# The second attention read in float32, one head per 32 columns of TensorE

## The chip, the cores and the metric

The kernel runs on one core of a Trainium2 chip. The time is device time in microseconds (us) of one execution. A core has TensorE (PE in the profile; its weight loads are PEld), VectorE (DVE), ScalarE (ACT), GpSimd (POOL) and SyncE (SP), whose queue issues the DMAs. Each engine has its own list of instructions and runs it in order; semaphores hold an instruction until what it needs is done.

## The reference

An attention between a sequence x and a small state, in both directions, and then a feed-forward layer:

```python
B, H, S, Ns, D = 8, 8, 512, 32, 64
a = softmax(scale * x @ state.T)          # over the 32 state rows
xread = a @ state
a2 = softmax(scale * state @ x.T)         # over the 512 positions
sread = a2 @ x                            # the second read: 32 x 64 per head
attn = concatenate([xread, sread], axis=2)
h = relu(attn_as_rows @ w_in)             # 512 -> 2048
out = (h * h) @ w_out                     # 2048 -> 512
```

attn_as_rows has 8 x 544 = 4352 rows of 8 heads x 64 = 512. All is float32 outside; w_in and w_out come as float64 and are decoded on the chip.

## The kernel before

**Blocks.** There are nine blocks of rows: block b from 0 to 7 holds the 512 x-read rows of batch b, block 8 the 256 state-read rows of all batches. For a block, hidden (16 steps) makes 128 of the 2048 hidden features each, and accumulate (16 steps) multiplies them by w_out into four accumulators in PSUM, one per 128 rows (tag acc, four buffers; two for block 8, from another pool). The state is multiplied into w_in beforehand, so hidden takes the softmax itself (k) as its moving operand.

**Split operands.** Most matmuls take operands in the type float32r as a high part (a cast on ACT) and a low part (a subtraction on DVE or POOL, as the table SECOND says); mm3 then adds three products, high by high, high by low and low by high. Blocks 0 and 1 (b < NX = 2) do parts of the attention in plain float32 instead.

**The second read.** A batch has two groups g of four heads, with 4 x 32 = 128 state rows on the partitions. For a group:

- scores: the scores in PSUM, with the four heads' states as a block-diagonal stationary operand; exp_s: e2, the exponentials (128 x 512), with the row sums, and r2, the reciprocals of the sums.
- load_n: loads x of the four heads with positions on the partitions (xn, tag xp, two buffers) and, for b >= 2, splits it into xn_hi and xn_lo (tags x_hi and x_lo, one buffer each, which prep uses too). There the buffer of xn is free when the split is done.
- transposes: four PE transposes of e2 into PSUM (pt, pool ps_b with two buffers), then to SBUF: a float32 copy eT for b < 2, a split into eT_hi and eT_lo for the others.
- sread: four position slices k. The stationary operand is the slice of eT (128 positions x 128 rows, four heads side by side), the moving one all four heads of xn (256 columns). The result pr is 128 x 256, of which only the four diagonal blocks (head by the same head) are used. For b < 2 these are four float32 matmuls, for the others mm3 with twelve. Four scalings by r2 on ACT pick the diagonal blocks into srd, and a DVE transpose writes them to srall, the input of block 8.

**The order.** The text PLAN lists the steps; a step's instructions are issued in that order, and the framework's scheduler (`TileContext(nc, schedule_with_timeline_sim=True)`) then writes each engine's list by estimates of durations, so that an engine's list may depart from the plan. A tile with a tag waits for one of that tag's buffers. The tag xp has two buffers, shared by x for prep (load), by xn (load_n), by the partial sums of blocks 0 and 1 (load_part, one tile for accumulators 0 and 1, one for 2 and 3), and at the end by half of the weights of block 8 (load_wi). These DMAs are issued from SP's queue. For block 1 the plan has load_n.2.0, load_n.2.1, sread.2.0, load_part.1, sread.2.1 and then the last two accumulates of block 1, whose sums are added to the parts in store (L812).

Of the kernel before, what the change touches and what calls it, by code (L numbers as in the profile page):

```python
# [10 lines left out]
F32 = mybir.dt.float32  # L11
F32R = mybir.dt.float32r
# [206 lines left out]
def tile_attn_moe(  # L219
# [31 lines left out]
    nc = tc.nc  # L251

    w_in_w, w_out_w = w_in.bitcast(U32), w_out.bitcast(U32)
    B, H, S, D = x.shape
# [3 lines left out]
    P = 128  # L258
# [7 lines left out]
    NX = 2  # L266
    LAG = 2
    second = set()
    for line in SECOND.replace("\n        ", " ").split("\n"):
        kind, _, keys = line.strip().partition(": ")  # L270
# [4 lines left out]
    KC = S // P  # L275

    cp = ctx.enter_context(tc.tile_pool(name="cp", bufs=1))
    p2 = ctx.enter_context(tc.tile_pool(name="p2", bufs=2))
    ps_acc = ctx.enter_context(tc.tile_pool(name="ps_acc", bufs=4, space=bass.MemoryType.PSUM))
    ps_h = ctx.enter_context(tc.tile_pool(name="ps_h", bufs=2, space=bass.MemoryType.PSUM))  # L280
    ps_b = ctx.enter_context(tc.tile_pool(name="ps_b", bufs=2, space=bass.MemoryType.PSUM))
# [17 lines left out]
    def pick(key, *engs):  # L299

        return engs[key in second]

    def split(hi, lo, src, key):

        nc.scalar.copy(hi, src)  # L305
        pick(key, nc.gpsimd, nc.vector).tensor_sub(lo, src, hi.bitcast(F32))  # L306

    def split_v(hi, lo, src):
        nc.scalar.copy(hi, src)
        nc.vector.tensor_sub(lo, src, hi.bitcast(F32))  # L310

    def evac(key, out, src):
        if key in second:
            nc.vector.tensor_copy(out, src)
        else:
            nc.scalar.copy(out, src)
# [5 lines left out]
    def mm3(ps, pairs, first=True, last=True, pin=False, skip=False):  # L322

        seq = []
        for (lh, ll), (rh, rl) in pairs:
            seq += [(lh, rh), (lh, rl), (ll, rh)]
        for i, (l, r) in enumerate(seq):
            m = nc.tensor.matmul(  # L328
                ps, l, r, start=first and i == 0, stop=last and i == len(seq) - 1, skip_group_check=skip
            )  # L330
            if pin:
                tc.keep_in_program_order(m)
# [29 lines left out]
    class Attention:  # L362
# [113 lines left out]
        def load_n(self, g):  # L476
            b = self.b
            x_v = x[b, 4 * g : 4 * g + 4].rearrange("h (p k) d -> p h (k d)", k=KC)
            if b < NX:
                xn = p2.tile([P, KC, 4, D], F32, tag="xp", name=f"xn{b}_{g}")  # L480
                for k in range(KC):
                    nc.sync.dma_start(xn[:, k], x_v[..., D * k : D * k + D])
                self.xn[g] = xn
                return
            xn = p2.tile([P, 4, KC, D], F32, tag="xp", name=f"xn{b}_{g}")
            nc.sync.dma_start(xn.rearrange("p h k d -> p h (k d)"), x_v)
            xnhi = p2.tile([P, 4, KC, D], F32R, tag="x_hi", name=f"xn_hi{b}_{g}", bufs=1)
            xnlo = p2.tile([P, 4, KC, D], F32R, tag="x_lo", name=f"xn_lo{b}_{g}", bufs=1)
            split(xnhi, xnlo, xn, f"xn_lo.{b}.{g}")
            self.xn[g] = (xnhi, xnlo)  # L490

        def transposes(self, g):
            b, e2 = self.b, self.e2.pop(g)
            pt = ps_b.tile([P, KC, P], F32, tag="psb", name=f"pt{b}_{g}")
            for k in range(KC):
                nc.tensor.transpose(pt[:, k], e2[:, k], ident)  # L496
            if b < NX:
                eT = p2.tile([P, KC, P], F32, tag="eT_hi", name=f"eTf{b}_{g}", bufs=1)
                evac(f"eT.{b}.{g}", eT, pt)
                self.eT[g] = eT  # L500
                return
            eThi = p2.tile([P, KC, P], F32R, tag="eT_hi", name=f"eT_hi{b}_{g}", bufs=1)
            eTlo = p2.tile([P, KC, P], F32R, tag="eT_lo", name=f"eT_lo{b}_{g}", bufs=1)
            split_v(eThi, eTlo, pt)
            self.eT[g] = (eThi, eTlo)

        def sread(self, g):

            b = self.b
            eT, xn, r2 = self.eT.pop(g), self.xn.pop(g), self.r2.pop(g)  # L510
            pr = ps_b.tile([P, 4, D], F32, tag="psb", name=f"pr{b}_{g}")
            prf = pr.rearrange("p h d -> p (h d)")
            if b < NX:
                for k in range(KC):
                    nc.tensor.matmul(prf, eT[:, k], xn[:, k].rearrange("p h d -> p (h d)"), start=k == 0, stop=k == KC - 1)
            else:
                mm3(
                    pr,
                    [((eT[0][:, k], eT[1][:, k]), (xn[0][:, :, k], xn[1][:, :, k])) for k in range(KC)],
                )  # L520
            srd = p2.tile([P, 2, 32], F32, tag="srd", name=f"srd{b}_{g}")
            for h in range(4):
                q = slice(32 * h, 32 * h + 32)
                nc.scalar.mul(srd[q].rearrange("p e d -> p (e d)"), pr[q, h], r2[q])  # L524
            nc.vector.transpose(srall[:, 2 * g : 2 * g + 2, b * Ns : b * Ns + Ns], srd)


# [465 lines left out]
    for k in PLAN.split():  # L993
        f, args, after = steps[k]
# [34 lines left out]
```

## Time and profile before

| | us |
|---|---|
| runs of the kernel (3) | 718.09, 719.53, 720.15; median 719.53 |
| the profiled execution | 718.72 |
| its span (first to last instruction) | 716.9 |
| granted clock of TensorE, mean share of full | 0.993 |

The profile is of one execution. A group of instructions is named by line, engine, operation and out<-in, with buffer numbers left out. Matmuls are pipelined and their ends are modelled: the starts say more than the durations. L328 is the matmul in mm3 and stands for many uses, so the tile's name tells them apart; pr is the second read's result.

| second read, before | instructions | first to last start, us |
|---|---|---|
| matmuls, blocks 0 and 1 (L515) | 32, 128x256 | 23.3 to 138.7 |
| matmuls, blocks 2 to 7 (L328, three products) | 3 x 48, 128x256 | 197.8 to 584.9 |
| scalings on ACT (L524) | 64, 32x64 | 26.7 to 586.1 |

### The profile page before, as it was taken

How to read it: one execution, taken by the hardware profiler on the slowest of the kernel's cores; microseconds unless marked ns; L12 is line 12 of the kernel's file. 1: busy time of each engine (PE TensorE's matmuls, PEld its weight loads, DVE VectorE, ACT ScalarE, POOL GpSimd, SP SyncE). 2: the span in 40 equal slices, each digit the busy share in tenths (PEclk: the TensorE clock that was granted, in tenths of full speed). 3: DMA queues.
4: the chain of work that ended last, by engine and by line, in shares of the span. 5: the costliest groups of instructions: out<-in, count | busy, mean ns of one | idle time of the engine just before them, and what ended most of it. 6: DMA issues, size and time to landing. Idle time of an engine off the chain costs nothing.

```text
span 716.9 us, 9806 instructions
## 1 busy us (share of the span) xinstructions
PE 688.5 (96%) x3281; PEld 571.7 (80%) x3281; DVE 422.0 (59%) x745; ACT 407.7 (57%) x798; POOL 145.0 (20%) x132
## 2 busy tenths in 40 slices
PE   5789699999999999999999999999999999999997
PEld 4567488878788888878888888888888888888886
DVE  4899989699665666766635574467348332322232
ACT  4586855777675656547645565557456553334323
POOL 1221601334202324423320230114003010000000
PEclk9999899999999999999999999999999999999999
DMA  9836477655765443565516354554355234434402
GB/s 274 218 105 222 154 250 240 214 181 160 256 193 182 164 161 104 189 203 170 166 49 203 103 164 156 195 176 162 89 176 160 75 102 141 141 113 115 126 0 89
DMA packets 94866, 113.64 MB, mean 159 GB/s; under 512 B 25952, under 2 KB 64864, under 8 KB 94816
## 3 DMA queue, kind: packets, MB, share of 16 engines
q1 hardware_dynamic: 94816, 113.02, 50.2%
q8 instruction: 26, 0.43, 0.3%
q14 instruction: 24, 0.20, 0.1%
HBM read 70.52 MB, written 42.47 MB: 158 GB/s over the span
## 4 chain that ended last, share of the span: by engine, by line
PE 79%; DVE 7%; DMA 6%; ACT 3%; issue 2%; SPq 2%; POOL 1%; DVEq 0%; ACTq 0%; POOLq 0%
PE acc L328 45%; PE ph L328 24%; PE pr L328 2%; PE st L328 2%; DMA wo_raw<-in_moe_w_out_dram 2%; PE w2ps L328 2%; DMA out_dram<-o 1%; PE qps L728 1%; PE qps L729 1%; DMA w_f<-w2p_d 1%; DMA xp<-in_x_dram 1%; SPq L685 1%; DVE dec L344 1%; DMA wi_raw<-in_moe_w_in_dram 1%; PE pt L496 1%
## 5 line engine op out<-in xcount | busy, mean ns | idle before, releaser
L328 PE MATMUL acc<-wo,g_hi 128*128 128x512 f32 x1088 | 315.9, 392 | 0.7 <-ACT g_hi L786 0.5
L328 PEld LDWEIGHTS acc<-wo,g_hi 128*128 128x128 f32 x1088 | 201.9, 188 | 42.3 <-ACT g_hi L786 0.9
L328 PE MATMUL acc<-wo,g_lo 128*128 128x512 f32 x544 | 187.9, 391 | 0.0
L328 PE MATMUL ph<-k_hi,w 128*128 128x512 f32 x512 | 181.6, 395 | 5.7 <-DVE g_lo L791 5.6
L791 DVE TENSOR_TENSOR g_lo<-ph,g_hi 128x512 fp32r<-128x512 f32 (+1 forms) x140 | 91.6, 655 | 102.7 <-ACT g_hi L786 101.4
L328 PEld LDWEIGHTS ph<-k_hi,w 128*128 128x128 f32 x512 | 96.5, 189 | 27.6 <-DVE g_lo L791 7.4
L328 PEld LDWEIGHTS acc<-wo,g_lo 128*128 128x128 f32 x544 | 101.0, 188 | 19.8
L786 ACT CAST g_hi<-ph 128x512 fp32r<-128x512 f32 (+1 forms) x144 | 81.1, 564 | 42.8 <-DVE ph L785 32.3
L328 PE MATMUL ph<-k_lo,w 128*128 128x512 f32 x256 | 100.5, 393 | 0.0
L785 DVE SCALAR_TENSOR_TENSOR ph<-ph,r 128x512 f32<-128x512 f32 (+1 forms) x76 | 49.9, 656 | 70.2 <-ACT r L784 70.2
L784 ACT ACTIVATE r<-ph 128x512 f32<-128x512 f32 (+1 forms) x76 | 43.1, 567 | 74.7 <-PE ph L328 74.3
L780 ACT ACTIVATE ph<-ph 128x512 f32<-128x512 f32 (+1 forms) x68 | 38.5, 568 | 53.2 <-PE ph L328 52.6
L328 PEld LDWEIGHTS ph<-k_lo,w 128*128 128x128 f32 x256 | 48.6, 190 | 9.2
L306 POOL TENSOR_TENSOR w<-w_f,w 128x512 fp32r<-128x512 f32 x23 | 30.1, 1309 | 93.0 <-ACT w L305 89.8
L781 ACT ACTIVATE ph<-ph 128x512 f32<-128x512 f32 (+1 forms) x68 | 38.6, 569 | 1.2
L306 POOL TENSOR_TENSOR x_lo<-xT,x_hi 128x512 fp32r<-128x512 f32 x11 | 14.3, 1303 | 111.1 <-ACT x_hi L305 99.0
L305 ACT CAST w<-w_f 128x512 fp32r<-128x512 f32 x40 | 24.6, 616 | 10.5 <-DMA w_f<-w2p_d 6.0
L622 PE MATMUL w2ps<-dec,bd 128*128 128x256 f32 x64 | 17.2, 419 | 11.6 <-DVE dec L344 8.6
L524 ACT ACTIVATE srd<-pr,r 32x64 f32<-32x64 f32 x64 | 19.6, 306 | 12.3 <-PE pr L328 9.5
L328 PE MATMUL ph<-sr_hi,s 128*128 128x256 f32 x128 | 25.5, 282 | 0.0
L622 PEld LDWEIGHTS w2ps<-dec,bd 128*128 128x128 f32 x64 | 12.9, 209 | 15.0 <-ACT bd L552 8.3
L306 POOL TENSOR_TENSOR xn_lo<-xn,xn_hi 128x1024 fp32r<-128x1024 f32 x7 | 16.8, 2400 | 36.1 <-ACT xn_hi L305 32.2
(134 smaller groups left out, 919.4 us busy)
## 6 DMA issues: line engine op xcount, KB each, us to landing
wi_raw<-in_moe_w_in_dram SPq DMA_DIRECT2D x16, 512.0 KB, 4.6
wo_raw<-in_moe_w_out_dram SPq DMA_DIRECT2D x16, 512.0 KB, 5.2
w_d<-qo SPq DMA_DIRECT2D x64, 128.0 KB, 2.1
out_dram<-o SPq DMA_DIRECT2D x32, 256.0 KB, 3.3
w_f<-w_d SPq DMA_DIRECT2D x32, 256.0 KB, 3.2
win_d<-wi SPq DMA_DIRECT2D x16, 512.0 KB, 3.3
w<-w2a_d SPq DMA_DIRECT2D x32, 256.0 KB, 3.9
s<-win_d SPq DMA_DIRECT2D x128, 64.0 KB, 2.0
```

What stands on the lines that cost most here:

```text
L305: nc.scalar.copy(hi, src)
L306: pick(key, nc.gpsimd, nc.vector).tensor_sub(lo, src, hi.bitcast(F32))
L328: m = nc.tensor.matmul(ps, l, r, start=first and i == 0, stop=last and i == len(seq) - 1, skip_group_check=skip)
L344: nc.vector.scalar_tensor_tensor(v, low, 29, v, ALU.logical_shift_right, ALU.bitwise_or)
L524: nc.scalar.mul(srd[q].rearrange("p e d -> p (e d)"), pr[q, h], r2[q])
L622: nc.tensor.matmul(ps[:, b], bd_f[b][:, 2 * g + c], w[:, c], start=first_c, stop=c == 1, skip_group_check=True)
L780: nc.scalar.activation(ph, ph, AF.Relu)
L781: nc.scalar.activation(ph, ph, AF.Square)
L784: nc.scalar.activation(r, ph, AF.Relu)
L785: nc.vector.scalar_tensor_tensor(ph, ph, 0.0, r, ALU.max, ALU.mult)
L786: nc.scalar.copy(ghi, ph)
L791: nc.vector.tensor_sub(glo, ph, ghi.bitcast(F32))
```

## The change

Three parts, for all blocks alike:

- load_n no longer splits xn: the float32 tile itself is kept for the read.
- transposes ends with one float32 copy eT (on ACT, or on DVE where SECOND lists it: 0.1 and 1.0 alone) for all blocks.
- sread makes, for each slice k and each head h, one float32 matmul: 32 columns of eT stationary, the 64 columns of that head moving, into the 32 partitions of pr that belong to the head. tile_position=(0, 32 * h) puts each into its own 32 columns of the array. pr is now 128 x 64, and one scaling by r2 takes the place of four.

```diff
-            xnhi = p2.tile([P, 4, KC, D], F32R, tag="x_hi", name=f"xn_hi{b}_{g}", bufs=1)
-            xnlo = p2.tile([P, 4, KC, D], F32R, tag="x_lo", name=f"xn_lo{b}_{g}", bufs=1)
-            split(xnhi, xnlo, xn, f"xn_lo.{b}.{g}")
-            self.xn[g] = (xnhi, xnlo)
+            self.xn[g] = xn
...
-            if b < NX:
-                eT = p2.tile([P, KC, P], F32, tag="eT_hi", name=f"eTf{b}_{g}", bufs=1)
-                evac(f"eT.{b}.{g}", eT, pt)
-                self.eT[g] = eT
-                return
-            eThi = p2.tile([P, KC, P], F32R, tag="eT_hi", name=f"eT_hi{b}_{g}", bufs=1)
-            eTlo = p2.tile([P, KC, P], F32R, tag="eT_lo", name=f"eT_lo{b}_{g}", bufs=1)
-            split_v(eThi, eTlo, pt)
-            self.eT[g] = (eThi, eTlo)
+            eT = p2.tile([P, KC, P], F32, tag="eT_hi", name=f"eT{b}_{g}", bufs=1)
+            evac(f"eT.{b}.{g}", eT, pt)
+            self.eT[g] = eT
...
-            pr = ps_b.tile([P, 4, D], F32, tag="psb", name=f"pr{b}_{g}")
-            prf = pr.rearrange("p h d -> p (h d)")
-            if b < NX:
-                for k in range(KC):
-                    nc.tensor.matmul(prf, eT[:, k], xn[:, k].rearrange("p h d -> p (h d)"), start=k == 0, stop=k == KC - 1)
-            else:
-                mm3(
-                    pr,
-                    [((eT[0][:, k], eT[1][:, k]), (xn[0][:, :, k], xn[1][:, :, k])) for k in range(KC)],
-                )
+            pr = ps_b.tile([P, D], F32, tag="psb", name=f"pr{b}_{g}")
+
+            for k in range(KC):
+                for h in range(4):
+                    q = slice(32 * h, 32 * h + 32)
+                    xh = xn[:, k, h] if b < NX else xn[:, h, k]
+                    nc.tensor.matmul(pr[q], eT[:, k, q], xh, start=k == 0, stop=k == KC - 1, tile_position=(0, 32 * h))
             srd = p2.tile([P, 2, 32], F32, tag="srd", name=f"srd{b}_{g}")
-            for h in range(4):
-                q = slice(32 * h, 32 * h + 32)
-                nc.scalar.mul(srd[q].rearrange("p e d -> p (e d)"), pr[q, h], r2[q])
+            nc.scalar.mul(srd.rearrange("p e d -> p (e d)"), pr, r2)
             nc.vector.transpose(srall[:, 2 * g : 2 * g + 2, b * Ns : b * Ns + Ns], srd)
```

## The prediction

> **What bounds the kernel now.** I read the page's busy shares first, then the table by stretches, then the waits.
>
> ```profile
> span 716.9 us, 9806 instructions
> PE 688.5 (96%) x3281; PEld 571.7 (80%) x3281; DVE 422.0 (59%) x745; ACT 407.7 (57%) x798; POOL 145.0 (20%) x132
> PE 79%; DVE 7%; DMA 6%; ACT 3%; issue 2%; SPq 2%; POOL 1%; DVEq 0%; ACTq 0%; POOLq 0%
> ```
>
> The first line is the span, the second busy time by engine, the third the chain that ended last by engine. TensorE (PE) is busy 96% of the span and is 79% of the chain. A share is an average over stages, so the table by stretches comes next: length, then busy time and instructions of PE, its weight loads (PEld), DVE, ACT and POOL, then granted clock and DMA.
>
> ```profile
> 0.00:60.00 60.00, 44.69 (x180) 32.73 (x181) 46.39 (x101) 37.36 (x84) 12.90 (x18) 0.97 0.72 208
> 60.00:185.00 125.00, 117.35 (x527) 95.35 (x526) 109.63 (x196) 88.90 (x173) 38.47 (x36) 0.97 0.60 198
> 185.00:590.00 405.00, 403.26 (x1947) 338.27 (x1946) 232.11 (x391) 238.43 (x456) 93.65 (x78) 1.00 0.49 156
> ```
>
> Only in the first 60 us is PE not the fullest engine. From 185 to 590 us it is busy 403.26 of 405 us at a granted clock of 1.00, while DVE and ACT are under 60%. The waits of PE inside that stretch are two rows (waiter, releaser, us in total, times, longest):
>
> ```profile
> PE qps L728 <- ACT qo L316: 1.3, 1, 1.3
> PE acc L328 <- DVE o L314: 0.2, 1, 0.2
> ```
>
> So there only PE time counts: 1.5 us of waiting is all that a lighter ACT, DVE or POOL could give back. The view of the tile pr, the result of the second read, shows where its work lies (ns least/median/most, first and last start in us):
>
> ```profile
> L524 ACT ACTIVATE srd<-pr,r x64: 299/307/310, 26.7 to 586.1; 32x64 f32<-32x64 f32 x64
> L328 PE MATMUL pr<-xn_hi,eT_hi x48: 277/283/287, 197.8 to 584.6; 128*128 128x256 f32 x48
> L515 PE MATMUL pr<-xn,eTf x32: 377/379/634, 23.3 to 138.7; 128*128 128x256 f32 x32
> ```
>
> The split form (L328, with as many for each of its other two products) runs from 197.8 to 584.6 us, wholly in the stretch that PE fills. The float32 form of blocks 0 and 1 (L515) lies in the first 139 us.
>
> **The change part by part: the PE time of one second read.** There are 12 split ones (blocks 2 to 7, two groups each) and 4 in float32.
>
> ```profile
> 197.80 0.28 PE L328 MATMUL pr<-xn_hi,eT_hi 128*128 128x256 f32 x1
> 199.12 0.28 PE L328 MATMUL pr<-xn_hi,eT_lo 128*128 128x256 f32 x1
> 199.24 0.28 PE L728 MATMUL qps<-tt,s_hi 128*128 128x256 f32 x1
> 137.23 1.89 PE L515 MATMUL pr<-xn,eTf 128*128 128x256 f32 x8
> 138.76 0.58 PE L328 MATMUL st<-x_hi,bd_hi 128*128 128x512 f32 x1
> ```
>
> A row gives start, duration, engine, line and count. The first two rows are the first and last of the 12 matmuls of a split read, the third is the next work: 199.24 - 197.80 = 1.44 us, 0.12 us for each. The end of a matmul, 0.28 us after its start, overlaps the next ones; 0.28 - 0.12 = 0.16 us is a tail. The fourth row is a float32 read: its four calls are x8, so one float32 matmul is two instructions. Eight starts lie in 1.89 us with a last duration of 0.38, so one comes each (1.89 - 0.38) / 7 = 0.215 us, and eight take 1.72 us.
>
> After the change each read is 16 float32 calls, 4 slices of the sequence by 4 heads, thus **32 instructions** with 64 columns moving instead of 256. In proportion one takes 0.215 x 64 / 256 = 0.054 us. The whole question is how many run side by side, and no row shows a matmul in part of the columns. From one side: four at once, 32 x 0.054 / 4 = 0.43 us. From the other: none beside another, 32 x 0.054 = 1.72 us. Between lies what the written order suggests: the two instructions of a call use the same 32 columns, one behind the other, and only the second can run beside the first of the next head. That gives 16 x 0.054 = 0.86 us, which I take.
>
> Weight loads and issue are other floors:
>
> ```profile
> 34.95 0.19 PEld L515 LDWEIGHTS pr<-xn,eTf 128*128 128x128 f32 x1
> 35.05 0.38 PE L515 MATMUL pr<-xn,eTf 128*128 128x256 f32 x1
> 21.94 0.14 PEld L496 LDWEIGHTS pt<-ident,e 128*128 128x128 f32 x1 [2.21 <-ACT e L444]
> 22.00 0.25 PEld L496 LDWEIGHTS pt<-ident,e 128*128 128x128 f32 x2
> ```
>
> A 128-column load leads its matmul by 0.10 us, so 32 columns need about 0.025 us (an estimate in proportion): 32 x 0.025 = 0.80 us, just under 0.86. After a wait of 2.21 us two loads, with a matmul between them, start 0.06 us apart; a pair can be issued at least that fast, and if this were a floor, 32 x 0.06 = 1.92 us is the upper end.
>
> Going from the whole array to column groups and back may cost something twice per read. The nearest row is another change of what the array does, from transposes to ordinary matmuls:
>
> ```profile
> 207.08 0.60 PE L496 MATMUL pt<-ident,e 128*128 128x128 f32 x4
> 207.44 0.48 PE L328 MATMUL ph<-k_hi,w 128*128 128x512 f32 x1
> ```
>
> The matmul behind four transposes starts 0.36 us after the first of them and is 0.08 us longer than the usual 0.40: nothing is lost there. The other end is two tails and one exposed load, 2 x 0.16 + 0.10 = 0.42 us. A transpose doesn't divide the array, so I don't take zero but one tail and one load, 0.26 us. So a read takes 0.86 + 0.26 = **1.12 us**.
>
> [...]
>
> **The sum.** Split reads: 12 x (1.12 - 1.44) = -3.8 us. Of the four float32 reads, those at 100.7 and 137.2 us lie in full PE work: 2 x (1.12 - 1.72) = -1.2 us. The other two don't count:
>
> ```profile
> 23.27 3.35 PE L515 MATMUL pr<-xn,eTf 128*128 128x256 f32 x8 [0.68 <-ACT eTf L316]
> 28.41 1.97 PE L622 MATMUL w2ps<-dec,bd 128*128 128x256 f32 x8 [1.79 <-DVE r L454]
> 35.05 1.89 PE L515 MATMUL pr<-xn,eTf 128*128 128x256 f32 x8
> 37.94 1.98 PE L419 MATMUL st<-xTf,bd 128*128 128x512 f32 x4 [0.99 <-ACT xTf L316]
> ```
>
> Behind each PE waits 1.79 and 0.99 us for DVE and ACT; a shorter read only lengthens that wait.
>
> Removed from other engines:
>
> ```profile
> L305 ACT CAST xn_hi<-xn x12: 1047/1050/1056, 191.5 to 572.3; 128x1024 fp32r<-128x1024 f32 x12
> L306 POOL TENSOR_TENSOR xn_lo<-xn,xn_hi x7: 2383/2399/2416, 192.7 to 573.4; 128x1024 fp32r<-128x1024 f32 x7
> L306 DVE TENSOR_TENSOR xn_lo<-xn,xn_hi x5: 1226/1226/1228, 200.6 to 515.5; 128x1024 fp32r<-128x1024 f32 x5
> L310 DVE TENSOR_TENSOR eT_lo<-pt,eT_hi x12: 673/692/694, 195.0 to 577.6; 128x512 fp32r<-128x512 f32 x12
> ```
>
> ACT loses 12 x 1.05 = 12.6 us, and three of the four scalings per read, 48 x 0.307 = 14.7 us (one of 128x64 taken at the price of 32x64). DVE loses 5 x 1.23 + 12 x 0.69 = 14.4 us, POOL 7 x 2.40 = 16.8 us. The cast of eT stays, as a plain copy. All of it lies beside full PE work, so I count 0, with 0 to -1.5 us (the waits above) as ends. The order in which the scheduler writes the lists will shift too: 0, ends ±1.5 us.
>
> One edit can cost. xn is no longer used up by its split but by the read itself, and it sits in one of two buffers (tag xp) that the partial sums of block 1 need:
>
> ```profile
> 200.56 1.23 DVE L306 TENSOR_TENSOR xn_lo<-xn,xn_hi 128x1024 fp32r<-128x1024 f32 x1
> 203.06 1.02 SPq L835 DMA_DIRECT2D part<-part_d  x2
> 225.96 0.28 PE L328 MATMUL pr<-xn_hi,eT_hi 128*128 128x256 f32 x1
> 228.04 1.28 DVE L812 TENSOR_TENSOR o<-acc,part 128x512 f32<-128x512 f32 x2
> 229.40 0.65 DVE L812 TENSOR_TENSOR o<-acc,part 128x512 f32<-128x512 f32 x1
> 230.37 0.62 PE L328 MATMUL acc<-wo,g_hi 128*128 128x512 f32 x2
> DMA to landing us min/median/max: 2.5/3.3/4.1
> ```
>
> Before, the buffer is free at 201.8 us and its loads (L835) go out at 203.06. After, it is free when the read that starts at 225.96 ends, about 227.2; two issues of 0.5 us and 3.3 us to landing make 230.6 and 231.1, and two adds of 0.65 us end at 231.3 and 231.9, about 2 us later than now. They free the third and fourth accumulators, which the next block's matmuls, from 230.37 on at 0.68 us per accumulator, reach at 231.7 and 232.4. The slack of 0.4 us is less than the spread of landings (2.5 to 4.1): I take +1.0 us, with ends 0 and 3.3. Behind these loads in SP's queue stand the stores and weight loads of the same stretch; the adds hold DVE's list.
>
> Sum: -3.8 - 1.2 + 1.0 = **-4.0 us**. The profiled execution took 718.72 us, 1.8 more than its span, and 0.8 less than the median of the runs, 719.53. So 714.7 against the profile, and 715.5 us as a median.
>
> **The rivals.** Break-even is where 12 x (c - 1.44) + 2 x (c - 1.72) + 1.0 = 0: a read of c = 1.41 us.
>
> First, **the column groups don't run beside each other** (the change doesn't do what it says). Then c = 1.72 + 0.26 = 1.98 us and the sum is 12 x 0.54 + 2 x 0.26 + 1.0 = +8.0: 727.5 us; with 1.92 + 0.42 it is 12 x 0.90 + 2 x 0.62 + 1.0 = +13.0, or 732.5. For it: the trace shows no overlap of two matmuls' streams, each waits for the one before. Against it: the heads share no column and no output partition. It decides from 44 ns per instruction on. [...]
>
> Second, **all four heads run at once**: c = 0.43 + 0.26 = 0.69 us, 12 x (-0.75) + 2 x (-1.03) + 1.0 = -10.1: 709.4 us; with free switches -14.4, 705.1. For it: independent columns. Against it: the two instructions of a call follow each other in one column group, and matmuls start in order.
>
> Third, **the switches at full price**: c = 1.28, -1.9 - 0.9 + 1.0 = -1.8, 717.7 us, which can't be told from no change (0.3%, 2.2 us, is about what a measurement of this kernel can tell).
>
> Fourth, on the slower side too: **the loads at L835 hold SP's queue** from 203.06 to 227.2 us. Weight loads wait behind them, and PE runs dry some 8 us (an estimate: a third of the 24 us held, since PE has two blocks' steps at hand): +3.0, 722.5 us. Against it: the lists are not bound to the written order. The plan puts this read ahead of block 1's last accumulate, yet block 1's first add had already started at 224.62 us, ahead of the read:
>
> ```profile
> 224.62 0.68 DVE L812 TENSOR_TENSOR o<-acc,part 128x512 f32<-128x512 f32 x1
> ```
>
> **How the numbers follow.** Forecast (c from 0.9 to 1.2): 0.35. All four at once: 0.13. Full price of switches, or c just under break-even: 0.15. No overlap: 0.30, of which 0.01 near zero. Queue held: 0.07. Faster 0.35 + 0.13 = 0.48; same 0.15 + 0.01 = 0.16; slower 0.29 + 0.07 = 0.36. Both signs hold much, so the forecast's own range is 711 to 718; the range for 8 in 10 goes from 706.5 (inside all four at once) to 730 (between the ends of no overlap).
>
> **What would show it.** In the profile after, PE has 32 matmuls of 64 columns per read, and the time from the first one's start to the start of what follows is c: near 1.1 us the forecast holds, over 1.41 it falls, near 0.7 the second rival is right. The first and last gaps show the switches. The busy time of ACT must fall by some 27 us, POOL's by 17, with no gain but the 1.5 us of waits. The loads at L835 show the buffer: their start, and whether PE waits for an add (L812). I would be wrong altogether if PE waited for something new elsewhere between 185 and 590 us.

## The result, and the profile after

The change makes the kernel slower: 729.08 us (median of 4 runs, 728.60 to 730.75) against 719.24 us for the kernel before on the same chip (718.09 to 720.15), a ratio of 1.0137 with a 95% interval of 1.0120 to 1.0154. The profiled execution took 729.16 us. The page of the changed kernel, with the same three lines as before: span, busy time by engine, chain by engine.

```profile
span 727.4 us, 10388 instructions
PE 684.7 (94%) x3617; PEld 558.5 (77%) x3617; DVE 402.7 (55%) x728; ACT 381.3 (52%) x738; POOL 128.2 (18%) x125
PE 75%; DVE 8%; DMA 7%; ACT 3%; SPq 2%; issue 2%; POOL 1%; DVEq 0%; ACTq 0%; POOLq 0%
```

ACT fell by 26.4 us and POOL by 16.8, about as worked out; DVE fell by 19.3, 4.9 more than worked out, since operations that stayed became shorter on average, too (k_lo<-aT,k_hi for one takes 689 ns in place of 903). PE is busy 3.8 us less but idle for 727.4 - 684.7 = 42.7 us, where it had been idle for 716.9 - 688.5 = 28.4 us: 14.3 us more idle, and so a span that is 10.5 us longer. Where, is told by the same table by stretches (length, busy time of PE, PEld, DVE, ACT and POOL, granted clock, DMA):

```profile
0.00:60.00 60.00, 40.80 (x214) 29.83 (x215) 43.49 (x93) 33.68 (x74) 13.41 (x18) 0.89 0.70 193
60.00:185.00 125.00, 108.92 (x524) 85.35 (x523) 105.89 (x192) 80.54 (x157) 34.86 (x33) 0.96 0.58 189
185.00:590.00 405.00, 401.72 (x2179) 329.89 (x2178) 216.70 (x382) 219.36 (x413) 79.97 (x74) 1.00 0.51 161
```

In the first stretch PE is busy 3.9 us less than before, in the second 8.4 us less, in the third 1.5 us less. So 12.3 of the 14.3 us of new idle time lie ahead of 185 us, where only 4 of the 16 reads are. The granted clock is lower there, too: by the trace's clock record PE's clock is at half speed for 23.9 us ahead of 185 us, where it had been for 10.2. PE works during 17.4 of these 23.9 us (before: 6.3 of 10.2) and loses half of that, 8.7 us in place of 3.1 (an estimate from the record: half the time at half speed, here and below). Without this its busy time would have fallen by some 9.4 us (an estimate: 3.8 and the 5.6 us of difference). The time at half speed differs between executions, but all four runs of the changed kernel have a mean granted clock of 0.981 to 0.983, and no run of the kernel before beside the experiments is under 0.986. The longest waits of PE from 60 to 185 us (waiter, releaser, us in total, times, longest), first in the kernel before and then in the changed one:

```profile
PE ph L328 <- DVE g_lo L791: 5.6, 1, 5.6
PE w2ps L320 <- ACT w L631: 0.7, 1, 0.7
PE acc L328 <- ACT g_hi L786: 0.5, 1, 0.5
```

```profile
PE ph L328 <- DVE g_lo L777: 8.7, 3, 5.6
PE acc L328 <- ACT g_hi L772: 3.9, 3, 2.7
PE acc L328 <- ACT po L316: 1.3, 1, 1.3
```

The waits for g_lo on DVE and g_hi on ACT, both of the feed-forward part, have grown from 6.1 to 12.6 us; none of them is the second read. The read itself is in the view of the tile pr (ns least/median/most, first and last start in us), and then in PE's timeline around its last execution:

```profile
L508 PE MATMUL pr<-xn,eT x512: 219/219/315, 22.6 to 594.7; 128*32 128x64 f32 x171
L510 ACT ACTIVATE srd<-pr,r x16: 309/315/318, 24.5 to 595.0; 128x64 f32<-128x64 f32 x16
```

```profile
591.70 0.39 PE L328 MATMUL acc<-wo,g_hi 128*128 128x512 f32 x1
591.93 0.39 PE L328 MATMUL acc<-wo,g_lo 128*128 128x512 f32 x1
...
593.97 0.39 PE L328 MATMUL acc<-wo,g_lo 128*128 128x512 f32 x1
594.29 0.65 PE L508 MATMUL pr<-xn,eT 128*32 128x64 f32 x32
594.87 0.50 PE L328 MATMUL ph<-k_hi,w 128*128 128x512 f32 x1
595.21 0.40 PE L328 MATMUL ph<-k_lo,w 128*128 128x512 f32 x1
```

All 32 matmuls lie in 0.65 us, the last being 0.22 long: (0.65 - 0.22) / 31 = 0.014 us from start to start, where 0.054 was worked out for one by itself. Four of these steps are 0.056 us, about the time of one by itself. So **all four heads run at once**. From its first start to the next work's, the prediction's measure, are 0.58 us. But the two neighbours step 0.23 us without a read (first two rows), and here they step 0.32 into the read and 0.34 behind it, which the split read doesn't cause; from 593.97 to 595.21 are 1.24 us, so the read takes 1.24 - 2 x 0.23 = **0.78 us in place of 1.44**. The last start of a read's matmul tells the sum: 594.7 us against 584.9 before, although twelve split reads are cheaper.

### The profile page after: what moved, and what is told of

It is laid out like the page before. It is cut to its first block, busy times and chain, and to the rows that moved or that the text cites. A ratio compares the mean times of both kernels' runs of the same rounds, so it can differ in the third digit from the quotient of the medians.

```text
span 727.4 us, 10388 instructions
## 1 busy us (share of the span) xinstructions
PE 684.7 (94%) x3617; PEld 558.5 (77%) x3617; DVE 402.7 (55%) x728; ACT 381.3 (52%) x738; POOL 128.2 (18%) x125
## 4 chain that ended last, share of the span: by engine, by line
PE 75%; DVE 8%; DMA 7%; ACT 3%; SPq 2%; issue 2%; POOL 1%; DVEq 0%; ACTq 0%; POOLq 0%
PE acc L328 43%; PE ph L328 23%; PE st L328 2%; DMA w_f<-w2p_d 2%; PE w2ps L328 1%; DMA wo_raw<-in_moe_w_out_dram 1%; PE pr L508 1%; DMA out_dram<-o 1%; DMA decq<-win_f 1%; DVE tt L704 1%; PE pt L493 1%; SPq L671 1%; DMA wi_raw<-in_moe_w_in_dram 1%; PE st L419 1%; DVE deco L343 1%
## 5 line engine op out<-in xcount | busy, mean ns | idle before, releaser
L328 PE MATMUL acc<-wo,g_hi 128*128 128x512 f32 x1088 | 319.1, 394 | 6.2 <-ACT g_hi L772 4.9
L328 PE MATMUL acc<-wo,g_lo 128*128 128x512 f32 x544 | 190.6, 392 | 0.0
L608 PE MATMUL w2ps<-dec,bd 128*128 128x256 f32 x64 | 18.9, 450 | 13.5 <-DVE dec L344 9.2
L384 DVE STREAM_TRANSPOSE xT<-xp 128x512 f32<-128x512 f32 x24 | 17.0, 706 | 23.0 <-DMA xp<-in_x_dram 18.8
L704 DVE TENSOR_TENSOR tt<-decq,tt 64x512 fp32r<-64x512 f32 x27 | 20.9, 775 | 5.1 <-ACT tt L700 4.3
```

The source lines that it names most:

```text
L328: m = nc.tensor.matmul(ps, l, r, start=first and i == 0, stop=last and i == len(seq) - 1, skip_group_check=skip)
L384: nc.vector.transpose(xT.rearrange("p (k j s) -> p k j s", k=KC, j=4), self.xp[g].rearrange("p (j k d) -> p k j d", j=4, k=KC)[..., 32 * e ...
L608: nc.tensor.matmul(ps[:, b], bd_f[b][:, 2 * g + c], w[:, c], start=first_c, stop=c == 1, skip_group_check=True)
L704: eng.tensor_sub(t[v, :, i], wf[u], t[u, :, i].bitcast(F32))
```

## The experiments

Theory: the read is cheaper, and the loss comes from the lists that the scheduler wrote anew, in which PE waits for ACT and DVE. Rival: the loss comes from column groups on the engine (switches, a lower clock, slower neighbours). Each run stands beside runs of the kernel before on its own chip.

| run | us, median | before there | ratio, 95% interval |
|---|---|---|---|
| e1_late_only | 717.29 | 720.08 | 0.9973 (0.9951 to 0.9995) |
| e2_early_only | 732.27 | 720.08 | 1.0173 (1.0150 to 1.0196) |
| e3_early_old_order | 719.73 | 719.22 | 1.0007 (0.9992 to 1.0022) |
| e4_full_old_order_185 | 722.45 | 719.22 | 1.0037 (1.0017 to 1.0057) |
| e5_own_xn_185 | 714.37 | 719.22 | 0.9921 (0.9891 to 0.9951) |
| e6_own_xn_370 | 710.58 | 719.22 | 0.9869 (0.9841 to 0.9897) |
| e7_first_read_only | 736.69 | 719.79 | 1.0239 (1.0213 to 1.0265) |
| e8_before_new_order | 731.38 | 719.79 | 1.0162 (1.0141 to 1.0183) |
| e9_xp_340 | 714.45 | 719.79 | 0.9924 (0.9906 to 0.9942) |
| e10_late_own_xn | 713.15 | 719.79 | 0.9908 (0.9889 to 0.9928) |
| e11_first_scalings_dve | 728.40 | 720.69 | 1.0110 (1.0081 to 1.0138) |
| e12_late_own_xn_370 | 710.79 | 720.69 | 0.9859 (0.9834 to 0.9884) |

**Late reads alone, early reads alone.** Each takes the change for some blocks and keeps the old code for the others, in load_n, transposes and sread:

```diff
 # e1_late_only, sread: the old read for blocks 0 and 1
+            if b < NX:
+                pr = ps_b.tile([P, 4, D], F32, tag="psb", name=f"pr{b}_{g}")
...
+                    nc.tensor.matmul(prf, eT[:, k], xn[:, k].rearrange("p h d -> p (h d)"), start=k == 0, stop=k == KC - 1)
...
+                return
 # e2_early_only, sread: the new read for blocks 0 and 1, the split one for the others
+            if b < NX:
+                pr = ps_b.tile([P, D], F32, tag="psb", name=f"pr{b}_{g}")
...
+                        nc.tensor.matmul(pr[q], eT[:, k, q], xn[:, k, h], start=k == 0, stop=k == KC - 1, tile_position=(0, 32 * h))
...
+                return
```

> The change for blocks 2 to 7 alone; blocks 0 and 1 read as before. In the changed kernel's trace a read occupies PE about 0.45 us and the switches about 0.25, so about 0.70 in place of 1.44. Theory (the loss comes from the order of work that the scheduler writes for the first 200 us, set off by the reads of blocks 0 and 1): the lists of the first 180 us are those of before, nothing is lost there, and the 12 reads save 12 x 0.74 = 8.9 us, less up to 1 for the held buffer: 710 to 712 us, faster. Rival (the held xp buffer or the column groups cost more elsewhere in PE's full stretch): slower than before, 720 to 730 us.

> The change for blocks 0 and 1 alone; blocks 2 to 7 read as before. Theory (order of the first 200 us): PE reaches 200 us some 13 to 15 us late as in the changed kernel and gains nothing later: 730 to 735 us, slower. Rival (the loss comes from blocks 2 to 7): 717 to 720 us, no change or slightly faster, since two reads of 1.72 us become 0.70.

e2 came out as its theory says. The two parts go opposite ways, -2.8 and +12.2 us, and their sum, +9.4, is about the +9.8 of the whole change: four reads lose everything, twelve gain, but less than their 12 x (0.78 - 1.44) = -7.9, and e1 is 5.3 us over the range of its theory. Of e1, the tile pr and the two longest waits of PE from 185 to 590 us:

```profile
L519 PE MATMUL pr<-xn,eT x384: 219/219/243, 200.8 to 586.2; 128*32 128x64 f32 x192
```

```profile
PE qps L725 <- ACT qo L316: 1.8, 1, 1.8
PE qps L725 <- DVE qo L314: 1.7, 2, 0.9
```

From its first to its last start lie 385.4 us, hardly less than the 386.8 from 197.8 to 584.6 of the kernel before: in this profile most of the reads' gain was given back in the same stretch. PE is idle there for 4.8 us (1.7 before), and 3.4 us at half speed, from 253.5 us on, cost another 1.7. The profile shows more loss than the median run: its execution took 720.24 us, 3.0 over the median.

**The early reads with the old lists.** A table ORDER gives, for each engine, the order of the kernel before as numbers of instructions in the plan's order (traced); at the end of the kernel function every instruction is bound to the one that precedes it in that table. This fixes the order of issue and adds no wait for a result. New instructions stand where the old read's stood. The table of e3 reaches to about 185 us, and the scheduler is free behind that; in the trace, the reads left aside, the lists of PE, ACT, DVE and POOL are those of the kernel before to the end.

```diff
+    for e, t in ORDER.items():
+        runs = [[int(v) for v in r.split("+")] for r in t.split()]
+        queue = [traced[e][j] for r in runs for j in range(r[0], r[0] + (r[1] if r[1:] else 1))]
+        for a, i in zip(queue, queue[1:]):
+            info = mybir.DependencyInfo(mybir.DependencyClass.NoSync, mybir.DependencyReason.DATA)
+            tc.add_manual_dep(i, a.name, info, reason="order")
```

> The column-group read for blocks 0 and 1 alone, as in the run before this (732.27 us), but every engine's list and the queue of SP are held in the order that they have in the kernel before, with the new read's instructions at the old read's place. Nothing else differs. Theory (the loss comes from the new order of the lists, and the read itself is cheaper): four reads go from 1.72 us to about 0.7 us, so 0 to 4 us under the kernel before, 715.5 to 719.5 us, and half-clock time near that of the kernel before. Rival (the loss comes from what the column groups do on the engine: a switch, a lower clock after them, slower neighbours): still slower, 728 us or more.

With the same four column-group reads and the old lists the time is the old one: 719.73 for 732.27 us, 0.2 over the range of the theory. The loss is gone, and so the rival falls. But the four reads, 1.72 - 0.78 = 0.94 us shorter each, gain nothing either. PE's timeline of this run at the first of them shows why:

```profile
22.43 0.65 PE L516 MATMUL pr<-xn,eTf 128*32 128x64 f32 x32 [0.68 <-ACT eTf L316]
27.56 3.75 PE L627 MATMUL w2ps<-dec,bd 128*128 128x256 f32 x8 [4.47 <-DVE r L454]
```

In the kernel before the wait behind this read was 1.79 us, and the eight matmuls of w2ps took 1.97 us in all. Now PE waits 4.47 us, and they run at half speed, 3.75 us. The work behind the read starts when DVE is done, whatever the read takes. The two later reads go the same way; the row of e3 from 60 to 185 us:

```profile
60.00:185.00 125.00, 115.20 (x567) 92.58 (x566) 108.38 (x193) 85.69 (x164) 38.76 (x36) 0.97 0.61 196
```

PE is idle for 9.8 us there, where it was idle for 7.65 in the kernel before; the two reads together are 1.9 us shorter.

**The new lists with no new read.** The same table, made from e2's lists, put on the kernel before:

> The kernel before with nothing of the change in it: every read is the old one. But all engines' lists and SP's queue are held in the order that the scheduler made for the kernel with the change in blocks 0 and 1 alone (732.27 us), with the old read's instructions at the new read's place. Theory (order alone): as slow as that kernel or a little slower, 731 to 737 us. Rival (the column-group reads are needed for the loss): 718 to 724 us.

Here the table holds the lists from start to end. The run has 731.38 us, 11.6 over the kernel before, with not one matmul in column groups. How far these lists are from the old ones can be counted in the traces, engine by engine, the reads left aside: of 4700 instructions on PE, ACT, DVE and POOL, 400 lie outside the longest order that both kernels have in common, as many in e2 as in e8. The first differ at about 31 us, just behind the first read; in e1 none differs ahead of 185 us. So **the order of the lists alone costs what the early reads cost**. The tile pr of e3, of e2 and of e8, the first product of the split reads each (first and last start):

```profile
L328 PE MATMUL pr<-xn_hi,eT_hi x48: 277/283/283, 198.1 to 584.9; 128*128 128x256 f32 x48
```

```profile
L328 PE MATMUL pr<-xn_hi,eT_hi x48: 277/283/283, 208.9 to 595.6; 128*128 128x256 f32 x48
```

```profile
L328 PE MATMUL pr<-xn_hi,eT_hi x48: 277/283/284, 210.3 to 597.0; 128*128 128x256 f32 x48
```

From the first to the last start there are 386.8, 386.7 and 386.7 us, as in the kernel before. With the new lists everything is lost ahead of the first late read, 10.8 and 12.2 us against e3.

**What sets the new lists off.**

```diff
 # e7_first_read_only: the new read for block 0, group 0 alone
+            if (b, g) == (0, 0):
 # e11_first_scalings_dve: the old kernel, the first read's four scalings on DVE
-                nc.scalar.mul(srd[q].rearrange("p e d -> p (e d)"), pr[q, h], r2[q])
+                eng = nc.vector.tensor_scalar_mul if (b, g) == (0, 0) else nc.scalar.mul
+                eng(srd[q].rearrange("p e d -> p (e d)"), pr[q, h], r2[q])
```

> One read alone, that of block 0, group 0, at 23 us of the span, is done with column groups and one scaling; the other 15 are those of the kernel before, and the scheduler is free. That one read can save 1.0 us at most and costs no more than a microsecond or so by itself. Theory (the loss is the new order of the lists, and the first read sets most of it off): 727 to 733 us, 8 us or more over the kernel before, lost before 200 us. Rival (each of the four early reads adds its share of the loss): 719 to 723 us.

> A control without any column group: the kernel before, with the four scalings of its first read (block 0, group 0) on DVE in place of ACT, which moves four instructions of some 0.3 us. The scheduler is free, and its lists move about as far from the kernel before as with the first read in column groups. Theory (these lists are tuned and any new order in the first 200 us costs, whatever set it off): 726 to 738 us. Rival (only the orders that a shorter read sets off are bad): 717 to 722 us.

One read of sixteen, changed alone, costs 16.9 us, more than all four together (and more than was expected). Four scalings of 0.3 us moved to DVE cost 7.7 us with no column group anywhere. Both lose it ahead of the late reads; the tile pr of e7, then of e11:

```profile
L328 PE MATMUL pr<-xn_hi,eT_hi x48: 277/283/283, 213.8 to 602.0; 128*128 128x256 f32 x48
```

```profile
L328 PE MATMUL pr<-xn_hi,eT_hi x48: 277/283/284, 207.2 to 595.3; 128*128 128x256 f32 x48
```

So the loss is no property of the new read; two quite different small edits at 23 us, by which the scheduler put some 210 (e7) and 280 (e11) instructions out of the old order, both cost 7.7 us or more. Which of the moved instructions cost the time, and whether SP's queue has a part in it, was not tried.

**The buffer of xn.** In the changed kernel the second pair of part loads goes out right behind the read that starts at 238.65 us, as predicted, and the third and fourth additions wait for them:

```profile
239.90 0.90 SPq L821 DMA_DIRECT2D part<-part_d  x2
243.28 0.69 DVE L798 TENSOR_TENSOR o<-acc,part 128x512 f32<-128x512 f32 x1 [1.02 <-DMA part<-part_d]
244.19 0.69 DVE L798 TENSOR_TENSOR o<-acc,part 128x512 f32<-128x512 f32 x1 [0.22 <-DMA part<-part_d]
```

The fourth rival, a held queue, didn't come true: from the first pair of these loads, at 212.85 us, to the second SP's queue issued other DMAs all along. Four runs have the whole change. e4 has the old lists up to 185 us and xn in xp, as the change has it. e5 is the same, but xn is loaded into the buffer in which its halves lay before:

```diff
-            xn = p2.tile([P, 4, KC, D], F32, tag="xp", name=f"xn{b}_{g}")
+            xn = p2.tile([P, 4, KC, D], F32, tag=("x_hi", "x_lo")[g], name=f"xn{b}_{g}", bufs=1)
```

e9 (xn in xp) and e6 (xn in x_hi and x_lo) hold PE, ACT, DVE and POOL up to 340 and 370 us, with SP's queue free.

> The whole change, with the lists of all engines and of SP held in the order of the kernel before up to about 185 us of the span; behind that the scheduler is free, as in the changed kernel. Theory (the main loss is the new order in the first 200 us, a smaller one of 3 to 4 us is the buffer of the xn tiles, which the part loads wait for): the gains of the 16 reads, 4 times up to 1.0 and 12 times 0.75, less 3 to 4 us, so 709 to 714 us. Rival (the order matters little, column groups cost elsewhere): 724 to 730 us.

> As the whole change with the old order up to 185 us, but the xn tile of blocks 2 to 7 no longer lies in the xp buffers: it is loaded straight into the x_hi or x_lo buffer, where its halves lay in the kernel before, so the part loads wait for no read. Theory (the wait of the part loads costs 3 to 4 us): 706 to 710 us, 3 to 4 us under the run with xn in xp. Rival (that wait is hidden, what was lost at 228 to 262 us is list order alone): within 1 us of the run with xn in xp, or slower, since the load of xn now waits for x_hi to come free.

> As the run with xn in x_hi and x_lo, but PE, ACT, DVE and POOL are held in the order of the kernel before up to about 370 us, and SP's queue is free from the start. Theory: what the scheduler's order loses between 185 and 370 us is kept too, so 704 to 709 us, the 16 reads' gain of 12 us against the kernel before nearly whole. Rival (the old order doesn't suit the new waits for x_hi, or SP's free order matters): 710 us or more.

> The whole change with xn in the xp buffers, where the part loads wait for the read; PE, ACT, DVE and POOL are held in the order of the kernel before up to about 340 us, SP's queue is free. Its twin with xn in x_hi and x_lo had 710.58 us. Theory (the buffer held until the read makes the additions of the parts late, whatever the order of the lists, and the engines queue behind them): 714 to 721 us, 4 us or more over the twin, lost between 225 and 260 us. Rival (only the order of the lists lost time there): within 2 us of the twin, 709 to 713 us.

With xn in xp, e4 came out 8 us over the theory; with xn elsewhere, e5 is 8.1 us faster than e4, twice what was expected. e5 and e6 are themselves 4.4 and 1.6 us over the ranges of their theories. Their tables by stretches, of e4 and then of e5, from 225 to 270 us:

```profile
225.00:270.00 45.00, 40.05 (x214) 33.17 (x213) 33.62 (x51) 25.22 (x46) 14.96 (x12) 0.92 0.67 213
```

```profile
225.00:270.00 45.00, 45.00 (x246) 37.67 (x246) 30.93 (x52) 25.35 (x47) 11.25 (x11) 1.00 0.54 170
```

In e4 PE is idle 4.95 us there, and the granted clock is 0.92. The timelines of PE, ACT and DVE of e4 give the chain:

```profile
241.94 0.28 PE L715 MATMUL qps<-tt,s_lo 128*128 128x256 f32 x1
247.17 0.55 PE L714 MATMUL qps<-tt,s_hi 128*128 128x256 f32 x1 [4.95 <-ACT qo L316]
...
250.73 0.41 PE L714 MATMUL qps<-tt,s_hi 128*128 128x256 f32 x1
250.94 0.41 PE L715 MATMUL qps<-tt,s_lo 128*128 128x256 f32 x1
```

```profile
244.95 0.58 ACT L772 CAST g_hi<-ph 128x512 fp32r<-128x512 f32 x1 [3.38 <-DVE ph L771]
...
246.43 0.60 ACT L316 COPY qo<-qps 128x512 f32<-128x512 f32 x1
```

```profile
243.62 0.71 DVE L384 STREAM_TRANSPOSE xT<-xp 128x512 f32<-128x512 f32 x1 [0.98 <-DMA xp<-in_x_dram]
244.25 0.67 DVE L771 SCALAR_TENSOR_TENSOR ph<-ph,r 128x512 f32<-128x512 f32 x1
```

PE waits for a copy on ACT; that copy stands in ACT's list behind a cast that waits for DVE; and what DVE makes for it stands behind a transpose that waited 0.98 us for a load into xp (another transpose of the same line had waited 2.65 us at 234.17). The matmuls of qps then start 0.21 us apart where they took 0.12 in the kernel before: half speed, which by the trace's clock record holds from 245.2 to 252.0 us. PE works for the last 4.9 us of it and loses half of them. 4.95 us of idle time and 2.4 lost to the clock are 7.4 of the 8.1 us. (SP's queue, held too in e4 up to 185 us, did wait for reads at the part loads, 5.3 us in two waits; the x loads behind them still went out at 228.46 us, in e5 at 229.25.) By the clock record of this trace the clock fell 3 us after PE's last matmul ended at 242.2 and came back 4.9 us after PE took up work.

Under the old lists the wait that the prediction described is there, but PE hardly meets it. The additions of the parts on DVE, in e9, then in e6:

```profile
228.78 0.68 DVE L798 TENSOR_TENSOR o<-acc,part 128x512 f32<-128x512 f32 x1
232.37 0.69 DVE L798 TENSOR_TENSOR o<-acc,part 128x512 f32<-128x512 f32 x1 [2.90 <-DMA decq<-win_f]
233.89 0.69 DVE L798 TENSOR_TENSOR o<-acc,part 128x512 f32<-128x512 f32 x1 [0.68 <-DVE srall L511]
```

```profile
226.18 1.28 DVE L798 TENSOR_TENSOR o<-acc,part 128x512 f32<-128x512 f32 x2
227.54 0.65 DVE L798 TENSOR_TENSOR o<-acc,part 128x512 f32<-128x512 f32 x1
```

In e9 the third addition, at 232.37 us, waits 2.90 us, and the last comes 6.4 us after that of e6. (The row names the DMA of decq; the part loads went out at 228.05 us and take 4.2 to landing in the median, which fits as well.) All the waits of PE in e9 from 190 to 280 us are these:

```profile
PE qps L714 <- ACT qo L316: 0.8, 1, 0.8
PE acc L328 <- ACT g_hi L772: 0.4, 1, 0.4
PE ph L328 <- DVE g_lo L777: 0.3, 1, 0.3
```

No addition is among them, and in e6 only the 0.4 us are left. So the expectation for e9 held about in size (3.9 us over its twin, or 3.3 with each against the kernel before on its chip) but not in place. PE is idle 0.9 us longer in e9 up to 185 us and 1.1 us longer from 185 to 280; what made the rest stays open, and SP's queue, free in both, isn't the same in them.

**What is left over.** The late reads alone with xn in x_hi and x_lo, without and with the old lists (up to 370 us):

> Blocks 2 to 7 with the column-group read, blocks 0 and 1 with the old one, xn of blocks 2 to 7 loaded straight into x_hi or x_lo, and the scheduler free: no list is held. Theory (the first 200 us keep the old order since the early reads are the old ones, the part loads wait for no read, 12 reads gain some 0.72 us each): 709 to 714 us, 4 to 8 us under the same with xn in xp (717.29). Rival (the scheduler's new lists behind 190 us lose as much as the buffer gives): 715 to 718 us.

> The column-group read in blocks 2 to 7 alone, xn in x_hi and x_lo, and PE, ACT, DVE and POOL in the order of the kernel before up to about 370 us. Its twin with the early reads in column groups too had 710.58 us, 0.9869 of the kernel before. Theory (the early reads' time is hidden by waits for DVE and ACT, so only 12 reads at some 0.72 us count): within 1.5 us of the twin, 709 to 712 us, ratio 0.985 to 0.990. Rival (the early reads gave part of the twin's gain): 712 to 715 us.

e10 needs no table of lists and has 713.15 us. PE's waits from 185 to 590 us in e10 are one row, and in e12, too:

```profile
PE acc L328 <- ACT g_hi L783: 0.6, 1, 0.6
```

```profile
PE acc L328 <- ACT g_hi L783: 0.4, 1, 0.4
```

e12, without the early column groups, is as fast as e6 with them: 0.9859 and 0.9869, each within the other's interval. So the early reads' time is hidden, as e3 said. e6 and e12, at 710.58 and 710.79 us, are the fastest; both beat the kernel before and the changed one.

## Why the prediction was wrong, point by point

Predicted were 715.5 us and faster; it is 729.08 and slower. It lies outside the forecast's own range, 711 to 718. That it lies inside the range for 8 in 10, 706.5 to 730, is luck: the upper end was drawn for column groups that don't overlap, which isn't what happened. With the measured read, 0.78 us, the prediction's sum would have been -8.8 in place of -4.0 us, further from the result.

- **The step that failed**: "The order in which the scheduler writes the lists will shift too: 0, ends ±1.5 us." The lists were rewritten from the first read on, and e8 measures that alone, for the early reads' lists, at 11.6 us. The argument looked at where PE is full, 185 to 590 us, and took for granted that the rest stays as it is; but the stretch ahead of it has 23 us of idle PE time, whose size hangs on the order in which ACT and DVE do their work: 35.3 us in the changed kernel, and 8.7 us lost to half speed in place of 3.1. The term was put at 0 without a reason.
- **The read.** c was taken as 1.12 us; it is 0.78. The second rival was right on the mechanism (four heads at once), with a dearer switch: 32 starts take 0.44 us, so entry and exit together take 0.34, where 0.26 was taken, between ends of 0 and 0.42. That these 0.34 us are the switches is the author's estimate; no row shows what takes them. 12 x (0.78 - 1.44) = -7.9 us instead of -3.8. Two figures of the rivals are off without bearing on the rest: with free switches the second rival's sum is -13.7 us, thus 705.8 us, not -14.4 and 705.1; and the 44 ns of the first rival leave out the 0.26 us of the switches, with which it is (1.41 - 0.26) / 32 = 36 ns.
- **The early reads**, "-1.2": 0, by e3. That the reads at 100.7 and 137.2 us lie in full PE work was wrong: PE is busy 94% from 60 to 185 us, but time saved there is time waited for DVE and ACT a little later. The reason that kept the first two reads out of the sum holds for all four.
- **The lighter engines**, "0 with 0 to -1.5": ACT and POOL fell as worked out and DVE by more, and in e6 and e12 the 1.5 us of PE's waits from 185 to 590 us have come down to 0.4.
- **The buffer**, "+1.0 us, with ends 0 and 3.3": 8.1 us between e4 and e5 on one chip; between e1 and e10 3.9 and between e6 and e9 3.3, each against the kernel before on its own chip. The named mechanism, late additions, is in the trace, but PE's waits from 185 to 590 us name no addition, in the changed kernel nor in e4 or e9 (a weight load waits 0.4 us for one in the changed kernel and 0.2 in e9). In e4 7.4 of the 8.1 us lie in one gap, in which PE's next work stands behind another engine's wait; that the scheduler wrote such lists because the buffer comes free late is likely, not shown, since e4 and e5 differ in both the buffer and the lists. It is a fault of both the size and the place.
- **The sum.** Against the kernel before: early lists +11.7 (e2 less e3), early reads themselves +0.5 (e3), late reads and the lighter engines -9.9 (e12), xn in xp and the late lists +7.1 (from e12 to e1: 3.26 to e10 for the late lists, 3.85 from there for the buffer with the lists that go with it). Together +9.4, which is e1 and e2 added, and the change measured +9.8. Of the -9.9, the reads are 7.9 and PE's shorter waits 1.1; the rest is within the interval of e12.

Of the things that would show the steps, the last one named decided, "if PE waited for something new elsewhere"; only elsewhere was ahead of 185 us, not behind it.

## What to carry to other kernels

Where a scheduler writes the lists by estimates, an edit of one early instruction is an edit of every list behind it: compare the lists of both kernels first, and price a stretch in which the fullest engine idles by its spread over orders (here 8 to 17 us), not at zero. To find out what an edit itself is worth, hold the old order around it, and put the new order on the old kernel; if the second run alone shows the loss, keep the edit and mend the order. And an operand that is no longer copied keeps its landing buffer until its last reader is done, so give it the buffer that the copy had.

## What the runs showed of the hardware that was not expected

- In the changed kernel four float32 matmuls in four groups of 32 columns run at once, though each call is two instructions: the 32 instructions of 64 columns of the read at 594.29 us start in 0.44 us, 14 ns apart on average, where 54 was estimated for one by itself. This excludes, for this kernel, the first rival, which decided from 44 ns per instruction on (36 with the switches).
- In e4 the half speed outlasted the idle gap of PE: 4.95 us idle, then 4.9 us of work at half speed. So this gap of 5 us cost 7.4 (an estimate: the 4.95 and half of the 4.9).
